# Sorted block attention and a token mixer on one core: first V regrouped, half of a q loaded in fp32, X of two batches turned by transposing transfers, another order

## The chip, the cores and the metric

The kernel runs on one core of one Trainium2 chip. A core has TensorE (PE), VectorE (DVE), ScalarE (ACT), GpSimd (POOL) and SyncE (SP), and 16 DMA engines that all queues share. The metric is device microseconds of one execution. A profiled execution has a span, from its first to its last recorded event, that is a little shorter than its time.

## The reference

```python
P = sort_net                                     # [4, 8, 8, 8]
for _ in range(5):
    P = exp(P - max(P, -1)); P = P / sum(P, -1); P = P / sum(P, -2)
k_sorted = einsum('bhij,bhjcd->bhicd', P, k_b)   # k, v: [4, 8, 768, 64], in 8 blocks of 96 rows
v_sorted = einsum('bhij,bhjcd->bhicd', P, v_b)
attn = softmax(q_block @ k_sorted_block.T / sqrt(64))      # inside each block of 96
x = (attn @ v_sorted_block)                      # to [4, 768, 512]
wq, wk = x @ w_q, x @ w_k                        # [4, 768, 64]
mixed = (wq @ wk.T / sqrt(64)) @ x
out = relu(mixed) @ w_out                        # [4, 768, 512] fp32
```

## The kernel before

Everything is kept on chip between the loads of q, k, v (four batches, 1.5 MB of fp32 each, cast to bf16 by Pool's transfers on the way) and the stores of `out`. Each engine runs its instructions in the order in which they are written, and that order is one hand-held list, the string ORDER. An entry is a letter for the step, a digit for the batch, then the part; after colons the engine (A ACT, D DVE, G Pool, S SyncE) and the PSUM bank. A capital letter is a step on TensorE (except D, R, N), the small letter the step that takes its result out of PSUM. So `Q21:0` turns part 1 of q of batch 2 into bank 0, and `q21:D` copies it to QT on DVE. Waits follow from the data, so an entry that waits holds all later entries of its engine, and of no other.

The steps, with the number of matmuls on TensorE:
- `a`, `c` (L171, L183): five rounds of the sinkhorn on 32x64 values, ACT and DVE in turn; `B` (L234) and `n` (L244) spread the result to the sort matrices M, by DVE for batch 0 and by Pool (1.3 us each) for the others. `Z` (L256): matmuls on zeros, no result.
- `l` (L220): loads, issued by Pool: `lq0` is q of batch 0, and `lq0b` its upper half. Three buffers each for q, k, v. `lp` the two small weights, `lo` w_out (wo).
- `Q` (12 matmuls) turns q; `K` (12) sorts and turns k. `S` (10, the last part 4) scores, `e` their exponentials E on ACT (L350).
- `V` (8, L303) sorts v into Vs; `R` (L313), a transfer by SyncE, regroups Vs from 6 rows per partition to blocks, in VT: six transfers per batch. In the kernel before, batch 0 goes without R: `Y` (12, L288) sorts v as K does, `y` copies it to a spare KT, `F` (8, L294) turns it back and `f` copies it to VT.
- `P` (14, the last part 8): attention times VT; `r` the reciprocals of the row sums, `x` (L378) the multiply that writes X, [96, 4 pairs of heads, 8 blocks, 128].
- `T` (8, L390) turns one quarter of X, `t` copies it to XT. `J` (4, L397) multiplies all four quarters of XT by w_q and w_k together: one J needs all of XT, for half of the columns. `j`, `d` (L405; by SyncE a transfer, by DVE a copy) put the results at qkT and qD.
- `W`, `G`, `H` (4 each for W and H, 8 for G): wk, the product wk.T @ x, then the mixed rows, two of six per H; `h` the relu into mixT.
- `O` (4 matmuls of 128x128x512, L453) one of six output rows; `o` its copy to `ot` (four buffers of two rows); `s` (L466) the store by SyncE, of two rows at once (512 KB) for batches 0 to 2 and of one (256 KB) for batch 3.

The function `u_D` (L386, `D`) writes half of XT by one transposing transfer; no entry of the order before uses it. With SPQ False, lines 128 to 132 and the first branch of `u_z` are not used either. After the last step Pool checks the row sums (L479) and falls back to a general path that does not run here.

Loads in the order before: q0, k0, v0, v1, k1, q1, the weights, q2, k2, v2, q3, k3, v3, w_out. The last batch ends with `O33:4 o33:A:4 s33:S`.

Of the kernel before, what the change touches and what calls it, by code (L numbers as in the profile page):

```python
# [12 lines left out]
ACT = mybir.ActivationFunctionType  # L13

NMIX = 2
SPQ = False
SPLIT = 6

ORDER = """
i02:D lq0 i00:G c00:D a01:A c01:D A00:0 a02:A:0 c02:D a03:A Z09:0 Q00:0 c03:D Q01:1 a04:A c04:D lk0  # L20
a05:A Q03:7 Q02:6 q01:A:1 c05:D Z06:2 B00:1 n00:D:1 n01:D:1 Z02:2 K00:2 K01:4 q00:A:0 k00:A:2
n02:D:1 u00:D:1 i03:G n03:D:1 K03:0 K02:2 k01:A:4 k02:D:2 k03:A:0 S00:4 S02:0 e00:A:4 q02:D:6 lv0
e02:A:0 Y02:2 q03:D:7 Y01:4 lv1 Y00:6 y01:D:4 Y03:0 y02:A:2 S04:2 y00:A:6 lk1 lq1 n10:G n11:G y03:D:0 S03:4
F01:6 F00:7 e04:A:2 S01:0 F03:2 e03:A:4 e01:A:0 f01:D:6 f00:D:7 V11:3 V12:5 f03:D:2 F02:7 P00:0
v11:A:3 v12:D:5 S05:2 f02:A:7 e05:A:2 r00:D:0 V10:4 n21:G P01:6 K13:2 x00:D:0 r01:D:6 P02:0
x01:D:6 v10:A:4 r02:D:0 K10:4 K12:6 k13:A:2 P03:2 x02:D:0 r03:D:2 k10:A:4 K11:4 k12:D:6 T01:0
T00:1 lp Q11:6 k11:A:4 t00:A:1 S06:4 U00:7 R12:S Q12:1 R15:S e06:A:4 R11:S x03:D:2 P04:2 t01:D:0
Q13:0 Q10:4 q11:A:6 r04:D:2 z01:A:7 S12:5 q12:D:1 x04:D:2 q13:A:0 U01:7 q10:D:4 z02:D:7 T02:1 T03:0
e12:A:5 t02:D:1 t03:D:0 lq2 S11:2 S10:4 S13:6 Q22:1 Q21:0 e11:A:2 q21:D:0 Q23:2 e10:A:4 q22:D:1
J00:3 e13:A:6 R10:S R14:S n20:G R13:S S16:4 e16:A:4 S15:0 j00:D:3 P11:6 S14:3 J01:5 e15:A:0 q23:D:2  # L30
e14:A:3 P12:0 r11:D:6 lk2 K23:2 j01:A:5 x11:D:6 K21:6 r12:D:0 P13:4 k23:A:2 K20:2 x12:D:0 k21:A:6
r13:D:4 n30:G K22:0 Q20:6 x13:D:4 W00:7 k20:A:2 lv2 k22:A:0 P14:2 lq3 V20:4 V22:0 d00:S q20:D:6
r14:D:2 W01:7 x14:D:2 V21:2 T12:6 v22:D:0 t12:D:6 v20:A:4 P10:4 S25:0 v21:A:2 S26:2 T13:6 r10:D:4
w00:A:7 T11:7 x10:D:4 d01:S e26:A:2 S23:2 n31:G e25:A:0 Q30:4 G00:5 S21:0 t13:D:6 e23:A:2 t11:D:7
S24:6 lk3 e21:A:0 G01:5 Q31:3 lv3 e24:A:6 g00:D:5 Q33:2 q31:D:3 S22:0 T10:5 e22:A:0 S20:6 q33:D:2
t10:D:5 K32:2 R21:S K31:0 J11:5 k32:A:2 R20:S q30:D:4 R22:S H00:2 Q32:4 e20:A:6 k31:D:0 lo j11:D:5
h00:A:2 R23:S K30:0 R24:S H01:6 q32:D:4 K33:4 h01:A:6 R25:S k30:D:0 P21:2 J10:0 V31:6 k33:A:4 P23:4
j10:A:0 v31:A:6 r21:D:2 P22:0 d10:S x21:D:2 r23:D:4 V32:2 W10:6 v32:A:2 W11:6 O01:7 x23:D:4 w10:A:6
V30:4 r22:D:0 v30:A:4 x22:D:0 o01:D:7 O02:2 S34:0 o02:D:2 H02:6 e34:A:0 h02:D:6 S32:3 O03:5 e32:A:3
o03:A:5 P20:0 T21:7 P24:2 r20:D:0 T22:4 t21:A:7 G10:5 G11:5 x20:D:0 r24:D:2 d11:S g10:D:5 S36:6  # L40
R32:S t22:A:4 S30:0 e36:A:6 R35:S O00:4 x24:D:2 S31:5 e30:A:0 R30:S H11:2 H10:0 O05:7 o00:D:4 T20:4
h11:D:2 o05:D:7 e31:A:5 R34:S T23:5 h10:A:0 t20:A:4 t23:A:5 S35:2 e35:A:2 R31:S S33:0 H12:6 e33:A:0
s01:S O04:4 J20:5 O10:3 s00:S j20:A:5 R33:S P31:0 J21:5 o10:A:3 P32:2 h12:D:6 O15:6 r31:D:0 o04:D:4
j21:A:5 r32:D:2 o15:A:6 x31:D:0 P33:4 r33:D:4 O12:7 o12:A:7 P30:0 x33:D:4 s02:S O13:6 d20:S P34:4
W20:7 x32:D:2 W21:7 r34:D:4 d21:S o13:A:6 T31:2 w20:D:7 O14:3 t31:D:2 r30:D:0 O11:7 G20:2 x30:D:0
G21:2 o11:A:7 s10:S x34:D:4 T30:7 o14:A:3 g20:A:2 t30:A:7 T32:0 T33:1 t32:D:0 t33:D:1 H21:4 H20:2
H22:6 h20:D:2 s11:S J30:0 J31:1 h22:D:6 O20:2 j30:D:0 O21:3 h21:A:4 W30:0 O22:7 j31:A:1 d31:D
w30:A:0 W31:0 o22:D:7 w31:D:0 O24:1 o20:A:2 o21:A:3 o24:A:1 G30:7 G31:7 g30:D:7 O23:0 d30:D H30:4
h30:A:4 o23:D:0 H31:2 s12:S h31:D:2 O25:7 s20:S H32:0 s21:S O31:4 o25:A:7 h32:D:0 O30:7 o31:D:4
s22:S s31:S O34:1 o34:A:1 o30:D:7 O32:4 O35:0 o32:A:4 s30:S o35:A:0 s34:S s32:S s35:S O33:4 o33:A:4  # L50
s33:S
"""


# [1 line left out]
def kernel(  # L56
# [12 lines left out]
    B, H, S, D = q.shape  # L69
    NB = sort_net.shape[-1]  # L70
    BLK = S // NB
# [7 lines left out]
    DM = moe_w_out.shape[0]  # L79
# [21 lines left out]
    def tiles(name, n, shape, dtype=BF16):  # L101
        return [sb.tile(shape, dtype, name=f"{name}{i}") for i in range(n)]

    PS = psp.tile([P, 8, 512], FP32, name="ps")
    ENG = {"A": nc.scalar, "D": nc.vector, "G": nc.gpsimd, "S": nc.sync}
# [13 lines left out]
    X = tiles("X", 2, [BLK, NP, NB, P])  # L119
    XT = tiles("XT", 2, [P, PT, S])  # L120
# [6 lines left out]
    ot = tiles("ot", NOT, [P, 2, DM], FP32)  # L127
    if SPQ:

        q32 = XT[0].rearrange("p t s -> p (t s)").bitcast(FP32).rearrange("p (h r d) -> p h r d", r=R6, d=D)  # L130
        nc.sync.dma_start(out=q32.rearrange("p h r d -> p h (r d)"),
                          in_=q[0, 0:H // 2].rearrange("h (p r) d -> p h (r d)", p=P))
# [251 lines left out]


    def u_D(b, n, e, bank):  # L386
        ENG[e].dma_start(out=XT[b % 2][:, 2 * n:2 * n + 2, :].rearrange("p k (i c) -> p (k i) c", c=BLK),
                         in_=X[b % 2][:, 2 * n:2 * n + 2].rearrange("c k i m -> c (k i m)"), transpose=True)

    def u_T(b, n, bank):  # L390
        for i in range(NB):
# [56 lines left out]
    def osplit(b, n):  # L448

        r, m = n % 10, n // 10  # L450
        return (r, slice(m * DM // 2, (m + 1) * DM // 2)) if b == B - 1 and r >= SPLIT else (r, slice(0, DM))

    def u_O(b, n, bank):  # L453
        r, c = osplit(b, n)
        for t in range(PT):
            mm(PS[:, bank, c], mixT[b % NMIX][:, t // 2, t % 2, r, :], wo[:, t, c],
               start=(t == 0), stop=(t == PT - 1))

    def oslot(b, n):
        return ot[(b * 3 + n // 2) % NOT]  # L460

    def u_o(b, n, e, bank):
        r, c = osplit(b, n)
        copy(e, oslot(b, r)[:, r % 2, c], PS[:, bank, c])

    def u_s(b, n, e, bank):  # L466
        od = out[b].rearrange("(p r) e -> p r e", r=R6)
        if b < B - 1:
            ENG[e].dma_start(out=od[:, 2 * n:2 * n + 2, :], in_=oslot(b, 2 * n))
        else:  # L470
            r, c = osplit(b, n)
            ENG[e].dma_start(out=od[:, r, c], in_=oslot(b, r)[:, r % 2, c])
# [172 lines left out]
    for item in ORDER.split():  # L645
# [5 lines left out]
        b, n = int(name[1]), int(name[2:])  # L651
# [41 lines left out]
```

## Time and profile before

| | us |
|---|---|
| median of 3 runs | 105.38 (105.36 to 105.59) |
| the profiled execution | 105.29 |
| its span | 103.5 |
| busy: PE, weight load, DVE, ACT, POOL | 86.7, 60.3, 71.8, 69.2, 25.4 |
| matmuls of O, 89 recorded | 22.8 busy, 380 ns each |
| copies to XT: ACT (6), DVE (10) | 808 and 544 ns each |
| regrouping transfers R, 18: issue on SP, to landing | 0.59 median; 2.3 to 7.5, median 6.2 |
| span over time in 40 slices, DMA busy | near full from 5 to 58 us, then 2 to 7 tenths |

PE's busy time counts each matmul with its pipeline, so a merged row of 16 matmuls is not twice as long as one of 8. The time to landing of a transfer runs from its issue to its last byte, and includes what stands ahead of it in its queue: the Pool's loads are issued some 10 to 25 us before they land, in one queue. A name such as VT stands for all buffers of that name.

### The profile page before, as it was taken

What the parts mean: (1) busy time and instruction counts of PE and PEld (TensorE: products, weight loads), DVE (VectorE), ACT (ScalarE), POOL (GpSimd) and SP (SyncE); (2) the same over time, 40 slices, a digit from 0 to 9 for tenths busy, and PEclk for the clock granted to TensorE, in tenths of its full rate; (3) what the DMA queues carried; (4) which work ended last, traced back from release to release, by engine and by line L of the source; (5) the groups of instructions that cost most, each with busy time, mean ns of one, the idle gap of its engine ahead of it and who ended that gap; (6) DMA issues with size and microseconds to landing.
All of it is one profiled execution on the core that took longest, in us unless ns stands there. A gap on an engine that the chain in (4) does not pass through costs nothing.

```text
span 103.5 us, 3508 instructions
## 1 busy us (share of the span) xinstructions
PE 86.7 (84%) x1485; PEld 60.3 (58%) x1493; DVE 71.8 (69%) x142; ACT 69.2 (67%) x98; POOL 25.4 (25%) x42
## 2 busy tenths in 40 slices
PE   0297977996959699999969899999999999999930
PEld 0135366895838577898745675856667575543410
DVE  2676667889956578989559498777389979368400
ACT  4222479998668868979849688989944282633440
POOL 5992054991199500000000000000000272000000
PEclk9999999999999999999999999999999999999999
DMA  0899999999999999999999933737042077047782
GB/s 3 88 199 204 204 204 205 203 206 203 237 232 244 206 202 204 209 210 206 241 247 228 208 77 100 224 142 255 6 176 65 6 301 307 24 185 301 299 321 99
DMA packets 18593, 19.35 MB, mean 187 GB/s; under 512 B 912, under 2 KB 16656, under 8 KB 18576
## 3 DMA queue, kind: packets, MB, share of 16 engines
q0 software_dynamic: 13296, 10.09, 63.6%
q1 hardware_dynamic: 5280, 9.03, 25.2%
q8 instruction: 11, 0.18, 0.7%
q14 instruction: 6, 0.05, 0.1%
HBM read 20.19 MB, written 6.29 MB: 256 GB/s over the span
## 4 chain that ended last, share of the span: by engine, by line
PE 44%; DMA 39%; POOL 6%; ACT 3%; SPq 2%; issue 2%; POOLq 0%; ACTq 0%
PE ps L156 44%; DMA Kn<-in_k_dram 18%; DMA Vn<-in_v_dram 14%; DMA VT<-Vs 7%; SPq L314 2%; POOL Vn L231 2%; POOL M L252 1%; POOL Qn L231 1%; ACT Vs L160 1%; POOL Kn L231 1%; ACT KT L160 1%; ACT ot L160 1%; POOL E L211 1%; ACT wk L160 0%; POOL VT L217 0%
## 5 line engine op out<-in xcount | busy, mean ns | idle before, releaser
L352 ACT ACTIVATE E<-ps 96x960 bf16<-96x960 f32 (+1 forms) x28 | 23.9, 905 | 2.9 <-PE ps L156 2.9
L156 PE MATMUL ps<-wo,mixT 128*128 128x512 bf16 x89 | 22.8, 380 | 0.5 <-issue 0.2
L381 DVE TENSOR_TENSOR X<-ps,Rall 96x896 bf16<-96x896 f32 (+1 forms) x20 | 19.9, 1001 | 0.5
L160 ACT COPY ot<-ps 128x512 f32<-128x512 f32 (+1 forms) x16 | 9.2, 587 | 8.6 <-PE ps L156 8.0
L160 ACT CAST KT<-ps 128x768 bf16<-128x768 f32 x14 | 10.6, 806 | 4.9 <-PE ps L156 4.9
L156 PEld LDWEIGHTS <-mixT 128*128 128x128 bf16 x96 | 8.3, 98 | 9.1 <-issue 1.0
L484 POOL CROSS_LANE_REDUCE s<-Rall 96x1 f32<-96x280 f32 x1 | 0.8, 756 | 46.5 <-DVE Rall L376 46.5
L156 PE MATMUL ps<-VT,E 96*128 96x65 bf16 x256 | 11.4, 193 | 0.8 <-DMA VT<-Vs 0.7
L156 PEld LDWEIGHTS <-E 96*128 96x128 bf16 x256 | 9.9, 97 | 3.1 <-issue 0.8
L252 POOL TENSOR_TENSOR M<-PTR,m_p 128x512 bf16<-128x512 bf16 x6 | 7.8, 1314 | 11.6 <-PE ps L156 6.0
L156 PEld LDWEIGHTS <-KT 64*128 64x128 bf16 (+1 forms) x288 | 8.3, 97 | 3.5 <-issue 2.2
L156 PE MATMUL ps<-QT,KT 64*128 64x96 bf16 x256 | 9.2, 204 | 0.4 <-ACT KT L160 0.3
L156 PE MATMUL ps<-idb,Qn 128*64 128x128 bf16 x192 | 7.1, 221 | 2.6 <-DMA Qn<-in_q_dram 2.6
L446 DVE TENSOR_SCALAR mixT<-ps 128x1024 bf16<-128x1024 f32 x7 | 8.5, 1220 | 1.2 <-PE ps L156 0.7
L156 PE MATMUL ps<-M,Kn 128*64 128x128 bf16 x192 | 7.2, 221 | 2.4 <-DMA Kn<-in_k_dram 1.8
L376 DVE RECIPROCAL Rall<-ps 96x14 f32<-96x14 f32 (+1 forms) x20 | 4.6, 231 | 6.7 <-PE ps L156 5.5
L156 PEld LDWEIGHTS <-Qn 128*64 128x64 bf16 x192 | 5.9, 110 | 4.0 <-DMA Qn<-in_q_dram 3.3
L156 PEld LDWEIGHTS <-Kn 128*64 128x64 bf16 x192 | 6.0, 109 | 3.7 <-DMA Kn<-in_k_dram 2.6
L160 ACT CAST Vs<-ps 128x1024 bf16<-128x1024 f32 x7 | 7.1, 1014 | 1.4 <-PE ps L156 1.2
L162 DVE COPY QT<-ps 128x768 bf16<-128x768 bf16 x12 | 6.3, 545 | 2.0 <-PE ps L156 2.0
L162 DVE CAST KT<-ps 128x768 bf16<-128x768 f32 x6 | 5.6, 942 | 2.8 <-PE ps L156 2.8
L162 DVE COPY ot<-ps 128x512 f32<-128x512 f32 x9 | 6.0, 678 | 2.1 <-PE ps L156 2.1
(81 smaller groups left out, 132.1 us busy)
## 6 DMA issues: line engine op xcount, KB each, us to landing
out_dram<-ot SPq DMA_DIRECT2D x9, 512.0 KB, 2.9
Qn<-in_q_dram POOLq DMA_DIRECT2D x4, 768.0 KB, 16.3
Kn<-in_k_dram POOLq DMA_DIRECT2D x4, 768.0 KB, 17.6
Vn<-in_v_dram POOLq DMA_DIRECT2D x4, 768.0 KB, 14.8
VT<-Vs SPq DMA_DIRECT2D x18, 132.0 KB, 6.2
out_dram<-ot SPq DMA_DIRECT2D x6, 256.0 KB, 2.0
wo<-in_moe_w_out_dram POOLq DMA_DIRECT2D x1, 512.0 KB, 26.7
qD<-qkT SPq DMA_DIRECT2D x6, 48.0 KB, 2.3
```

The source lines that it names most:

```text
L156: nc.tensor.matmul(o, w, x, is_transpose=t, start=start, stop=stop, skip_group_check=True)
L160: nc.scalar.copy(o, i)
L162: nc.vector.tensor_copy(o, i)
L211: nc.gpsimd.memset(t[:, :, 2 * TH * BLK:EW], 0.0)
L231: nc.gpsimd.dma_start(out=t[b % NIN][:, h0:h1].rearrange("p h r d -> p h (r d)"), in_=src[b, h0:h1].rearrange("h (p r) d -> p h (r d)", p=P))
L252: ENG[e].tensor_tensor(out=M[b % 2][:, h0:h0 + hn], in0=src.unsqueeze(2).to_broadcast([P, hn, SP, NB]), in1=m_p.unsqueeze(1).unsqueeze(3). ...
L314: ENG[e].dma_start(out=VT[b % 2].rearrange("(s r) i h x -> r s i (h x)", r=R6)[n], in_=Vs[0][:, n].rearrange("p h e -> p (h e)"))
L352: nc.scalar.activation(E[b % 2][:, n, 0:2 * w * BLK].rearrange("p (t a c) -> p a t c", a=2, c=BLK), PS[0:BLK, bank:bank + 2, 0:w * BLK].re ...
L376: nc.vector.reciprocal(Rall[:, b, n, :, 0:w], avps(bank, w)[:, :, :, D])
L381: nc.vector.tensor_mul(xo.rearrange("p (a t d) -> p a t d", a=2, d=D), avps(bank, w)[:, :, :, 0:D], Rall[:, b, n, :, 0:w].unsqueeze(3).to_ ...
L446: nc.vector.tensor_relu(o, i)
L484: g.tensor_reduce(s1[:, 1:2], rv, axis=AX.XYZWC, op=ALU.max)
```

## The change

`SPQ` is set: SyncE loads the first four heads of q of batch 0 in fp32, into the space of XT of batches 0 and 2, before anything else but `sort_net`; `z11` and `z10` cast it on ACT to Qn, and Pool loads the other half (`lq0b`). Batch 0's v goes through `V` and `R` like the others, so `Y`, `F` and their copies are gone. `T` and `t` of batches 2 and 3 (eight of each) are gone; `D20`, `D21`, `D30`, `D31` on SyncE turn two quarters of X each. Stores of batches 0 and 1 go out by single rows (`ROWS`), and rows 0 and 1 of batch 3 by one store at the very end (`s320`). `SPLIT` splits nothing before or after. The whole order is another one.

```diff
-SPQ = False
-SPLIT = 6
+SPQ = True
+SPLIT = ()
+XK = 2
+ROWS = ((0, 0), (0, 1), (0, 2), (1, 0), (1, 1), (1, 2))
...
-i02:D lq0 i00:G c00:D a01:A c01:D A00:0 a02:A:0 c02:D a03:A Z09:0 Q00:0 c03:D Q01:1 a04:A c04:D lk0
...
+i02:D c00:D lk0 a01:A c01:D i00:G A00:2 a02:A:2 z11:A c02:D Z08:2 Q01:2 a03:A z10:A c03:D a04:A
+c04:D a05:A c05:D Q00:1 i03:G lq0b Z09:0 B00:5 n03:D:5 n00:D:5 lv0 n01:D:5 Z03:0 K00:3 k00:D:3 lq1
...
+n30:G V22:2 r12:D:0 v22:A:2 P10:4 S25:6 x12:D:0 J00:0 r10:D:4 x10:D:4 V21:2 e25:A:6 V20:4 j00:A:0
+v21:D:2 P13:0 K30:6 v20:A:4 k30:A:6 K31:2 r13:D:0 d00:S K33:4 x13:D:0 k31:A:2 K32:6 T12:0 P11:1
+k33:D:4 R20:S t12:D:0 P14:3 k32:A:6 S23:5 R25:S r14:D:3 x14:D:3 r11:D:1 J01:7 R22:S e23:A:5 j01:A:7
+W00:0 R21:S R23:S S24:3 Q30:5 x11:D:1 Q31:6 e24:A:3 W01:0 q30:D:5 T11:1 Q32:2 lv3 q31:A:6 T10:4
+w00:D:0 t11:A:1 T13:7 q32:D:2 S30:5 S21:2 S31:0 t13:D:7 R24:S G00:7 G01:7 t10:A:4 J10:4 e30:A:5
+g00:D:7 lo e21:A:2 e31:A:0 j10:D:4 J11:5 V30:2 j11:D:5 v30:A:2 V31:0 v31:D:0 d01:S V32:4 P24:2
+r24:D:2 H00:6 H01:0 R32:S v32:A:4 P20:4 x24:D:2 W10:2 h00:A:6 Q33:3 r20:D:4 h01:A:0 W11:2 P21:6
...
+G11:3 S35:1 R33:S g10:A:3 R35:S S34:6 R31:S P22:4 O00:3 d11:S r22:D:4 e34:A:6 e35:A:1 P23:6 O04:0
+x22:D:4 o00:A:3 R34:S r23:D:6 o04:A:0 x23:D:6 O05:3 H11:6 H10:0 o05:D:3 D20:S S33:4 h11:A:6 O01:2
+e33:A:4 P30:6 o01:A:2 h10:D:0 P31:0 D21:S r31:D:0 s00:S P32:4 O03:2 J20:3 o03:A:2 r30:D:6 s01:S
+x30:D:6 j20:A:3 O11:6 s02:S o11:A:6 r32:D:4 x31:D:0 W20:3 x32:D:4 J21:0 d20:S P33:1 j21:A:0 d21:S
+S36:6 H12:4 W21:3 e36:A:6 w20:A:3 r33:D:1 x33:D:1 O12:0 P34:6 h12:A:4 G20:3 G21:3 O13:4 o13:A:4
+o12:D:0 r34:D:6 O14:5 D30:S g20:A:3 x34:D:6 D31:S O10:6 o14:A:5 H20:0 H21:2 h20:A:0 o10:D:6 s11:S
+H22:4 O15:7 h21:A:2 J31:6 j31:D:6 d31:D h22:A:4 s10:S o15:D:7 J30:1 O22:3 j30:D:1 W31:6 O23:2 W30:1
...
+O35:7 o33:A:0 o32:A:1 s33:S s32:S o35:A:7 O31:1 s35:S o31:A:1 o34:D:6 O30:7 s34:S o30:A:7 s320:S
...
-        ENG[e].dma_start(out=XT[b % 2][:, 2 * n:2 * n + 2, :].rearrange("p k (i c) -> p (k i) c", c=BLK),
-                         in_=X[b % 2][:, 2 * n:2 * n + 2].rearrange("c k i m -> c (k i m)"), transpose=True)
+        t = slice(XK * n, XK * n + XK)
+        ENG[e].dma_start(out=XT[b % 2][:, t, :].rearrange("p k (i c) -> p (k i) c", c=BLK),
+                         in_=X[b % 2][:, t].rearrange("c k i m -> c (k i m)"), transpose=True)
...
-        if b < B - 1:
-            ENG[e].dma_start(out=od[:, 2 * n:2 * n + 2, :], in_=oslot(b, 2 * n))
+        if b < B - 1 or n >= 20:
+            m = 2 * (n % 20)
+            w = 1 if (b, n) in ROWS else 2
+            for r in range(0, 2, w):
+                ENG[e].dma_start(out=od[:, m + r:m + r + w, :], in_=oslot(b, m)[:, r:r + w, :])
```

The loads come in the order k0, upper half of q0, v0, q1, k1, v1, q2, k2, the weights, v2, k3, q3, v3, w_out.

## The prediction

> **What bounds the kernel now.** I read the chain of waits first, in order of time.
>
> ```profile
> 6.63 18.26 DMA Kn<-in_k_dram
> ...
> 29.34 14.51 DMA Vn<-in_v_dram
> ...
> 49.73 7.52 DMA VT<-Vs
> ...
> 86.39 6.24 PE ps L156 x51
> 92.62 0.16 issue
> 92.78 6.56 PE ps L156 x31
> ```
>
> Start, length, what. Until 57.26 the chain goes from landing to landing; from there it is TensorE in pieces without a gap worth naming. Busy time by engine in three windows cut at that place says the same.
>
> ```profile
> 0.00:57.30 57.30, 45.22 (x984) 34.92 (x985) 41.88 (x96) 41.80 (x58) 22.22 (x35) 1.00 1.21 199
> 57.30:99.40 42.10, 41.43 (x501) 25.34 (x508) 29.90 (x46) 26.78 (x40) 3.22 (x7) 1.00 0.51 172
> 99.40:103.50 4.10, 0.00 (x0) 0.00 (x0) 0.00 (x0) 0.59 (x1) 0.00 (x0) 0.95 0.44 168
> ```
>
> Columns: window and length, busy PE, weight load, DVE, ACT, POOL, granted clock, DMA share, GB/s. In the first window TensorE is idle for 12.1 us and the transfers run at 199 GB/s (bytes as written; the casting loads read twice that). In the second it is idle for 0.7 us of 42.1 at clock 1.00. The third is the last copy and store. So three terms set the end: when the last operand lands, TensorE's work after that, and the tail.
>
> The waits of TensorE and the sizes and landing times of the transfers:
>
> ```profile
> PE ps L156 <- DMA Qn<-in_q_dram: 2.6, 3, 1.0
> PE ps L156 <- DMA Kn<-in_k_dram: 1.8, 2, 1.0
> PE ps L156 <- DMA VT<-Vs: 0.7, 1, 0.7
> ```
> ```profile
> out_dram<-ot SPq DMA_DIRECT2D x9, 512.0 KB, 2.9
> Qn<-in_q_dram POOLq DMA_DIRECT2D x4, 768.0 KB, 16.3
> VT<-Vs SPq DMA_DIRECT2D x18, 132.0 KB, 6.2
> out_dram<-ot SPq DMA_DIRECT2D x6, 256.0 KB, 2.0
> ```
>
> **The stream of loads, priced.** Issue plus time to landing of each load gives: Q0 9.0, K0 12.85, V0 16.6, V1 20.8, K1 24.9, Q1 29.5, the two small weights 30.9, Q2 35.8, K2 39.6, V2 43.9, Q3 47.8, K3 53.1, V3 58.35, wo 60.9. Undisturbed neighbours are 3.75 to 3.9 us apart (Q0 to K0, K0 to V0, Q2 to K2). From Q0 to V3 lie 11.17 loads in 49.4 us; 11.17 x 3.8 is 42.4, so 6.9 us went to the 12 regroupings (R) and two qD transfers among them, and to irregular steps (V0 to V1 took 4.2 with no R). I take 0.49 us for an R, 2.9 for six.
>
> **TensorE's items, priced** by how much longer a merged row is with one more of them (X turned: 8 matmuls 0.51, 16 0.85, 24 1.19, so 0.34 for a T): Q and K 0.33, V 0.46, S 0.21 (S.6 0.08), P 0.43 (P.4 0.25), T 0.34, J 0.65, W 0.17, G 0.43, H 0.23, O 0.865. From P21, which starts on the last landing at 57.39, the order before holds 10 P, 5 J, 3 V, 6 W, 24 O, 7 S, 10 H, 8 T, 6 G: 39.3 us. The trace took 41.95 (to 99.34). The factor is 1.067.
>
> **The change part by part.**
>
> *First V regrouped.* Four Y and four F (3.2 us of TensorE) and their eight copies (0.7 to 1.0 us each) become three V (1.4 us), three copies (1.0 to 1.2) and six R. The engine time saved lies in the first window, where TensorE has 12 us to spare: worth nothing now, and should the loads cease to bind, at most the 1.8 us of TensorE. The six R join the stream ahead of V3: +2.9 us. If the VT transfers filled only holes it would be 0, but the DMA share of 1.2 to 1.33 from 5 to 58 us shows none.
>
> *Half of the first q in fp32.* SP issues it second (about 1.15 us; the sort_net transfer issued at 0.75 landed at 2.3). The Pool stream moves its first bytes at 3.0 and full rate only at 5.0; until then it moved 0.19 MB, as if it had begun at 4.0. Half a load is 1.9 us of stream. Nearly all of it now runs in idle time: -1.5 us, bounds 0 (it merely shares) and -1.9. On ACT two casts to Qn (0.8 each, as the 128x768 copies) stand between the exponentials of the sinkhorn, where ACT idles 1.46 to 1.52 us per round. The first waits for the transfer, and the next exponential stands behind it; I expect landing near 5.9, so the matrix is some 0.4 us late. Its readers (M, then K00) then come at 13 instead of 12.5, against loads that are ahead of TensorE: hidden. Uncovered it would be 0.4. Pool issues K0 first and half of Q0 after the memsets: the same bytes.
>
> *Order.* V1 moves behind Q1 and K1, Q3 behind K3; V3 stays last but wo. TensorE now meets V30 where it met P21: VT of batch 2 is issued by 52.5 and lands, as before after about 7 us, near 59.5, when three V are still to run. V3 lands at 58.35 - 1.5 + 2.9 = 59.75. The work ahead of V30 is no later: from V22 (V2 lands near 45.0) to Q30 are 6.7 us of items, Q3 lands near 54.2, from Q30 to V30 are 5.0 x 1.067 = 5.3, which gives 59.5. Pool's four M products still stand ahead of loads; the last of them queue behind V12's reads of M, near 32 us, when 12 us of loads are in flight: hidden.
>
> *X of batches 2 and 3 turned by transposing transfers.* Eight T (2.7 us) and eight copies (0.55 DVE, 0.81 ACT) leave. From V30 the new order holds 3 V, 10 P, 12 H, 6 W, 1 Q, 24 O, 5 S, 6 G, 4 J: 36.3, x 1.067 = 38.7. TensorE would end at 98.5 instead of 99.34: -0.85, if nothing waits. Against it stands J, which needs all of XT. After x23, the multiply that D21 waits for, TensorE has work until J20 worth 4.5 x 1.067 = 4.8 us; after x34, from which D31 starts, 4.0 us (P34 to J31 holds 5.0 of items, x34 ends 1.6 after P34, J31's first two matmuls read the other half).
>
> No row shows a transposing transfer. It moves 384 KB on the chip in 1536 pieces of 256 B. Lower bound: as a store, between 2.0 (256 KB) and 2.6 (the quietest 512 KB), 2.4 us: no wait. Upper bound: every piece a load packet (63.6% of 103.5 us x 16 / 13296 = 79 ns), 96 per engine 7.6 us, and 2.0 to land: 9.6. The nearest row is R, the other on-chip regrouping: three R carry the bytes. Three issues of 0.588 and a landing of 2.35 (R on the quiet queue at 60 to 62 us) are 4.1; with the 4.3 that they took beside stores, 6.1. The queue is quiet here, so 4.6. D20 holds SP for some 1.76 us and starts D21 about 0.35 late: D21 is 4.6 + 0.35 - 4.8 = 0.15 late, D31 0.6: +0.75. The queue behind D20 and D21 holds stores and d20, d21, which wait for J anyway.
>
> The Trainium skill (Advanced Engine Details and Errata, X-Bar Transpose) says that transposing transfers are as fast as ordinary ones. By that rule the sum loses its 0.75. The Trainium skill (DMA: Bandwidth & Descriptors, the table of sequencer costs) counts 32 sequencer cycles per tile on earlier generations; 96 tiles of 16x128 at the 1.2 GHz of the clock table (Advanced Engine Details, Clock Domains) would be an estimate of 2.6 us of issue each, and with a landing of 2.35 the two waits together 2.2 instead of 0.75: 107.5. No run here shows either yet.
>
> *Stores.* Batches 0 and 1 go out by rows: six more issues of 0.33 us, on an SP queue that waits 5 us at a time for copies: hidden. The very last store becomes 512 KB instead of 256: 2.6 to 2.9 against 2.0, +0.7, at the end of everything.
>
> Sum: -0.85 + 0.75 + 0.7 = +0.6. The profiled execution took 105.29, 1.8 more than its span (the median is 105.38). 105.29 + 0.6, and a little for waits behind new neighbours: **106.0**.
>
> **Rivals.**
> - *Faster: transposes within their cover.* At up to 4.0 us neither J waits. With the other terms as above that is 105.14; with the first q fully ahead (-1.9), R at 0.35 (2.1) and the tail at 0.3, V3 lands at 58.55, TensorE ends at 97.3, and the time is 103.5. It decides where x34 to the landing of D31 is under 4.0. For it: the quiet queue after 62 us; against: 1536 small pieces. This is also where the skill's rule leads. 0.37 for a gain, 0.12 for 105.17 to 105.6.
> - *Slow transposes.* At 7 to 9.6 us D21 comes 2.5 to 5.1 late and D31 3.0 to 5.6: 111 to 116. For it: the packet price; against: that price belongs to loads that read 1536 B. 0.10.
> - *The stream is later than I add*, with q shared rather than ahead: V3 at 61.2, +1.5: 107.4, within my case.
> - *The change does nothing it says*: possible for the first two parts, which then cost and gain 0; the transposes still move T off TensorE. Within the range.
>
> **How the numbers follow.** The forecast case, slower by 0.2 to 3.5 us, holds 0.41; with slow transposes slower is 0.51. Measurements of this kernel tell about 0.2% apart, 0.2 us. Same 0.12, faster 0.37. Cases of both signs hold most of the chance: the forecast's own range is 105.6 to 108.9; the whole, leaving out the slow end of the transposes and the best end of the gain, 103.4 to 109.5.
>
> **What would show it.** Landing of V3 (59.75) and the first V30 matmul on it; TensorE busy without gaps from there except ahead of J20 and J31, with "DMA XT<-X" as releaser and 0.15 and 0.6 us; time to landing of XT<-X near 4.6; TensorE's last matmul near 99.3; last store to landing 2.6 to 2.9. Wrong would be: landing of XT far from 4.6, a wait of several us on VT or Qn after 60 us, or V3 before 58.4.

## The result, and the profile after

The changed kernel takes 106.6 us, median of 4 runs (106.43 to 107.49), against 105.37 of the kernel before beside it: ratio 1.0112, interval 1.007 to 1.0153. It is slower by a good 1%. The profiled execution took 106.43 with a span of 104.6; before it was 105.29 and 103.5.

The chain of waits after the change, its last part (start, length, what):

```profile
53.84 8.67 DMA VT<-Vs
62.51 0.24 issue
62.75 10.34 PE ps L156 x177
73.08 3.53 DMA XT<-X
76.61 0.04 issue
76.66 23.81 PE ps L156 x188
```

Before, the last landing on the chain was at 57.26. Now a VT landing at 62.5 and a transposing transfer stand on it, 5 us and 19 us later. The windows, cut where the first V of batch 3 begins on TensorE (60.27) and where TensorE ends (columns as before: window and length, busy PE, weight load, DVE, ACT, POOL, clock, DMA share, GB/s):

```profile
0.00:60.27 60.27, 47.09 (x936) 36.09 (x937) 38.31 (x88) 45.56 (x62) 22.18 (x35) 0.97 1.22 213
60.27:100.50 40.23, 39.03 (x442) 22.88 (x439) 26.73 (x42) 25.36 (x39) 3.22 (x7) 1.00 0.72 207
100.50:104.60 4.10, 0.00 (x0) 0.00 (x0) 0.00 (x0) 0.57 (x1) 0.00 (x0) 1.00 0.58 231
```

The same cut in the kernel before is at 58.67, where its first V of batch 3 begins:

```profile
58.67:99.40 40.73, 40.18 (x485) 24.43 (x489) 29.56 (x45) 26.15 (x39) 3.22 (x7) 1.00 0.48 171
```

So the 1.1 us are made up thus: V of batch 3 begins 1.6 us later; the part from there to TensorE's end is 0.5 shorter (40.2 for 40.7: 1.15 us less of work, 0.65 more of idle time); the tail is the same 4.1. The two stretches do not hold quite the same items: behind V30 there are eight T and two S fewer than behind the first V of batch 3 before, and a P, a Q and two H more. Of the 1.15 us of work saved, more than half came back as idle time. These are the waits of TensorE (us in total, times, longest):

```profile
PE ps L156 <- DMA Kn<-in_k_dram: 2.4, 1, 2.4
PE ps L156 <- ACT E L352: 1.2, 4, 0.4
PE ps L156 <- DMA VT<-Vs: 1.0, 1, 1.0
...
PE ps L156 <- DMA XT<-X: 0.2, 1, 0.2
```

The 1.0 and the 0.2 are the only named waits behind 60 us: P24 on VT of batch 2 (at 62.75) and J20 on the transposes (at 76.66). The 2.4 is K of batch 1, which keeps TensorE from 22.96 to 25.37 (before, it waited 0.84 for that load); its granted clock falls behind it. The time before V of batch 3 shows where the start was lost. From 20 to 50 us and from 50 to 60, before and then after:

```profile
20.00:50.00 30.00, 26.52 (x630) 22.52 (x628) 23.36 (x40) 25.02 (x33) 10.67 (x12) 1.00 1.30 214
50.00:60.00 10.00, 8.22 (x183) 6.14 (x180) 6.81 (x12) 7.53 (x10) 0.00 (x0) 1.00 1.22 227
```
```profile
20.00:50.00 30.00, 23.37 (x540) 19.80 (x542) 18.60 (x29) 24.60 (x32) 12.74 (x14) 0.94 1.28 222
50.00:60.00 10.00, 9.83 (x224) 8.11 (x224) 7.74 (x15) 9.35 (x13) 0.00 (x0) 1.00 1.26 231
```

Before, TensorE got 26.5 us done from 20 to 50 and had room from 50 to 60. After, it got 23.4 done and was full from 50 on: the work was pushed back and met V of batch 3 as a queue. Transfers, from issue to landing:

```profile
VT<-Vs SPq DMA_DIRECT2D x24, 132.0 KB, 6.4
...
XT<-in_q_dram SPq DMA_DIRECT2D x1, 768.0 KB, 4.5
...
XT<-X SPq DMA_TRANSPOSE x4, 3.8
```

Landings, issue plus time to landing: K0 9.6, half of Q0 11.5, V0 15.4, Q1 20.2, K1 25.3, V1 30.6, Q2 34.4, K2 39.0, V2 45.6, K3 49.6, Q3 53.2, V3 59.3, wo 62.7. Before, V2 came at 43.8, V3 at 58.4, wo at 60.9.

### The profile page after: what moved, and what is told of

Read it like the earlier page. It is cut to its first block, busy times and chain, and to the rows that moved or that the text cites. A ratio compares the mean times of both kernels' runs of the same rounds, so it can differ in the third digit from the quotient of the medians.

```text
span 104.6 us, 3280 instructions
## 1 busy us (share of the span) xinstructions
PE 86.1 (82%) x1376; PEld 59.0 (56%) x1376; DVE 65.0 (62%) x129; ACT 71.5 (68%) x100; POOL 25.4 (24%) x42
## 4 chain that ended last, share of the span: by engine, by line
PE 44%; DMA 30%; DVE 8%; POOL 5%; ACT 5%; issue 4%; SPq 1%; DVEq 0%; POOLq 0%; ACTq 0%
PE ps L156 44%; DMA Kn<-in_k_dram 18%; DMA VT<-Vs 8%; DVE X L381 4%; DMA XT<-X 3%; ACT KT L160 2%; DVE KT L162 2%; POOL Qn L231 2%; ACT E L352 1%; SPq L314 1%; POOL Kn L231 1%; ACT Vs L160 1%; DVE Vs L162 1%; POOL Vn L231 1%; DVE Rall L376 1%
## 5 line engine op out<-in xcount | busy, mean ns | idle before, releaser
L160 ACT CAST Vs<-ps 128x1024 bf16<-128x1024 f32 x10 | 10.0, 1018 | 2.4 <-PE ps L156 1.6
L156 PE MATMUL ps<-M,Kn 128*64 128x128 bf16 x192 | 8.0, 226 | 4.1 <-DMA Kn<-in_k_dram 2.4
L445 ACT ACTIVATE mixT<-ps 128x1024 bf16<-128x1024 f32 x8 | 7.9, 1023 | 3.8 <-PE ps L156 3.8
L162 DVE CAST KT<-ps 128x768 bf16<-128x768 f32 x8 | 7.5, 952 | 4.5 <-PE ps L156 4.5
L156 PE MATMUL ps<-idb,Qn 128*64 128x128 bf16 x192 | 8.4, 239 | 0.9 <-DMA Qn<-in_q_dram 0.7
L156 PEld LDWEIGHTS <-KT 64*128 64x128 bf16 x256 | 7.1, 99 | 3.7 <-issue 1.8
L160 ACT CAST KT<-ps 128x768 bf16<-128x768 f32 x8 | 6.1, 801 | 4.2 <-PE ps L156 4.2
L156 PEld LDWEIGHTS <-Qn 128*64 128x64 bf16 x192 | 6.6, 121 | 2.5 <-DMA Qn<-in_q_dram 0.9
L156 PE MATMUL ps<-fil 128*128 128x512 bf16 x20 | 6.5, 480 | 1.6 <-ACT m_p L174 1.6
L156 PE MATMUL ps<-Vn,M 128*128 128x128 bf16 x96 | 7.1, 219 | 0.9 <-ACT E L352 0.5
```

The source lines that it names most:

```text
L156: nc.tensor.matmul(o, w, x, is_transpose=t, start=start, stop=stop, skip_group_check=True)
L160: nc.scalar.copy(o, i)
L162: nc.vector.tensor_copy(o, i)
L445: nc.scalar.activation(o, i, ACT.Relu)
```

## The experiments

Each is timed beside the kernel before on the same chip (medians 105.44 for e1 to e4, 105.54 for e5 to e11, 105.65 for e12).

| run | us, median (range) | ratio to before | interval |
|---|---|---|---|
| the change | 106.6 (106.43 to 107.49) | 1.0112 | 1.007 to 1.0153 |
| e1, filler ahead of K10 | 106.07 (105.86 to 106.14) | 1.0054 | 1.0037 to 1.0071 |
| e2, change without R of batch 0 | 107.99 (107.5 to 108.96) | 1.0226 | 1.0195 to 1.0258 |
| e3, change with T on TensorE | 112.7 (112.64 to 112.84) | 1.0692 | 1.067 to 1.0714 |
| e4, change with q by Pool | 107.62 (107.12 to 108.61) | 1.0226 | 1.016 to 1.0293 |
| e5, e1 with V of batch 2 early | 106.58 (106.37 to 107.85) | 1.0105 | 1.007 to 1.014 |
| e6, e1 with a divided last store | 106.35 (106.03 to 107.42) | 1.0062 | 1.0032 to 1.0093 |
| e7, before with D20, D21 | 105.65 (105.42 to 106.27) | 1.0001 | 0.9973 to 1.0028 |
| e8, e7 with D30 | 105.71 (105.36 to 106.34) | 1.0003 | 0.9976 to 1.0031 |
| e9, before with half of q in fp32 | 105.02 (104.91 to 105.81) | 0.9964 | 0.9944 to 0.9984 |
| e10, before with six R too many | 107.79 (107.58 to 108.09) | 1.0216 | 1.0192 to 1.0241 |
| e11, e9 with D20, D21 | 104.08 (103.9 to 105.14) | 0.9886 | 0.9851 to 0.9921 |
| e12, e11 with D30 | 104.85 (104.58 to 105.7) | 0.9933 | 0.9906 to 0.9961 |

**e1: the clock behind the wait for K of batch 1.** Ten matmuls on zeros fill the wait (in the entry `Z010:5` the 10 is their number and the 5 the bank).

```diff
-K10:6
+Z010:5 K10:6
```

> The changed kernel with ten matmuls on zeros (Z) in the wait for K1, nothing else. Theory clock: in the changed kernel TensorE idles 2.4 us before K10 and its granted clock falls to 0.5 from about 27 to 30.6 us; the late V of batch 2, so its R and VT (landing 62.5), follow from that. Then the clock stays at 1.00, the items from K10 to P00 run some 1.8 us sooner, V1 (30.6) binds instead, and the time falls by 0.5 to 1.0 us, to 105.6 to 106.1, with less spread between runs. Theory stream: the six added R make the stream longer and that alone sets VT's landing. Then the clock is mended and the time stays within 0.2 us of 106.5.

The windows of the changed kernel around the wait; the number behind POOL is the granted clock:

```profile
23.00:24.00 1.00, 0.00 (x0) 0.00 (x0) 0.49 (x2) 1.00 (x3) 1.00 (x3) 1.00 1.23 241
24.00:25.00 1.00, 0.00 (x0) 0.00 (x0) 0.00 (x0) 0.88 (x2) 1.00 (x2) 1.00 1.21 248
...
27.00:28.00 1.00, 0.88 (x18) 0.83 (x20) 0.83 (x1) 0.33 (x2) 0.00 (x0) 0.56 1.21 245
28.00:29.00 1.00, 1.00 (x26) 0.83 (x24) 0.47 (x1) 0.91 (x2) 0.00 (x0) 0.50 1.33 215
29.00:30.00 1.00, 1.00 (x25) 0.86 (x22) 0.09 (x1) 0.69 (x2) 0.00 (x0) 0.50 1.29 199
30.00:31.00 1.00, 0.72 (x21) 0.58 (x16) 0.55 (x1) 1.00 (x2) 0.00 (x0) 0.73 1.34 207
```

and of e1:

```profile
24.00:25.00 1.00, 1.00 (x6) 0.47 (x5) 0.00 (x0) 1.00 (x2) 1.00 (x3) 1.00 1.23 250
...
28.00:29.00 1.00, 0.81 (x32) 0.60 (x28) 0.67 (x2) 1.00 (x2) 0.00 (x0) 1.00 1.32 215
```

With the gap filled the clock stays at 1.00, and the median is 0.5 us lower (the intervals of the two just meet, at 1.007). The five runs lie within 0.3 us, where the changed kernel's four spread over 1.1. But VT of batch 2 still lands at 62.4, so that landing does not hang on the clock. And in the profiled executions the mended clock is not seen behind the loads: V30 begins at 60.27 in the change and at 60.47 with the filler, and P24 at 62.75 in both. The two lines of e1:

```profile
60.47 1.50 PE L156 MATMUL ps<-Vn,M 128*128 128x128 bf16 x24
62.75 0.41 PE L156 MATMUL ps<-VT,E 96*128 96x65 bf16 x8 [0.77 <-DMA VT<-Vs]
```

TensorE ends 0.34 us earlier with the filler. All of that comes at J20, which waits for D21 in the change and not with the filler, where D20 held SyncE for 1.66 us instead of 2.28. The changed kernel's other three executions had mean clocks of 0.942 to 0.961 (the profiled one 0.984) and took 106.43 to 107.49 us. These three have no profile, so how much of the 0.5 us is the clock's stays open.

**e2: R of batch 0 taken out of the change** (Y, y, F, f of batch 0 in place of V, v, R).

```diff
-V02:0 v02:A:0 V01:2 v01:A:2
+Y02:0 y02:A:0 Y01:2 y01:D:2
...
-R03:S R05:S lv1
+lv1
...
-S03:0 R02:S R04:S e04:A:2 K10:6 q11:D:4
+S03:0 Y03:6 y03:D:6 e04:A:2 F02:5 f02:D:5 q11:D:4 F01:4 f01:D:4 F00:5 f00:A:5 F03:4 f03:D:4 K10:6
```

> The changed kernel with the first V regrouped on TensorE again (Y, y, F, f in place of V, v and six R of batch 0; the four F lie in the wait for K1). Theory stream: six R cost 2.9 us of stream, so Q1 to V3 land 2 to 3 us sooner, V3 near 56.5, VT of batch 2 near 59.5, and the time falls by 1.5 to 2.5 us, to 104 to 105, under the kernel before. Rival: the chain after K1 is bound by engines, not by the stream; then V3 lands sooner but the time falls by less than 0.8 us.

V3 landed at 56.9, 2.4 earlier, and V2 at 43.7, 1.9 earlier. Yet the time rose by 1.4: the eight steps were put by hand into an order searched without them, and TensorE waits 1.6 us for the copy to QT that now stands among theirs on DVE; its clock falls behind that wait too, from 25.9 to 29.3. The landing answers the price of the six R (2.4); the time does not answer what the part is worth.

**e3: transposes back on TensorE**, in the places of the transfers.

```diff
-D20:S
+T20:2 t20:D:2 T21:3 t21:A:3
...
-D31:S O10:6 o14:A:5
+O10:6 o14:A:5 T32:7 t32:A:7 T33:3 t33:D:3
```

> The changed kernel with the four transposing transfers undone: eight T on TensorE and eight copies. Theory: the transfers land 3.5 to 4.8 us after issue, inside their cover, and take 2.7 us off a TensorE that is busy throughout; undone, the time rises by 2.0 to 2.8 us, to 108.5 to 109.2. Rival, as forecast: waits at J eat part of that, then it rises by 1 to 1.9 us.

+6.1 us, more than either bound. From V30 to its last product TensorE takes 46.1 us instead of 40.2: 3.2 more of work, which is the eight T, and 2.7 more of idle time. The longest new wait is not that of a T:

```profile
88.16 1.02 PE L157 MATMUL ps<-wo,mixT 128*128 128x512 bf16 x4 [1.24 <-DVE X L382]
```

It is O10, which takes the bank that x34 has to read first, and x34 now stands on DVE behind the copy of a T. The run shows that the order of the change is laid out for transfers, and not what a T costs in an order made for it.

**e4: all of the first q by Pool.** `SPQ = False`, `lq0` in the place of `lk0` and `lk0` in that of `lq0b`, no `z10`, `z11`.

> The changed kernel with the whole first q loaded by Pool (cast on the way), ahead of k0, and no casts on ACT. Theory: the fp32 half is worth 1.5 us of stream; all landings come 1.5 us later (V1 32.1, V3 60.8), and the time rises by 0.7 to 1.5 us, to 107.2 to 108. Rival: the chain behind K1 is bound by engines; then the time rises by less than 0.4 us.

The loads from Q1 on land 0.5 to 1.0 us later (V2 46.3, V3 60.0, wo 63.7), and the time rises by 1.0. The fp32 half is worth 0.8 us of stream at V3, half of what the forecast gave it.

**e5: V of batch 2 early**, so that VT lands before P24 wants it.

```diff
-V22:2 r12:D:0 v22:A:2 P10:4 S25:6 x12:D:0 J00:0 r10:D:4 x10:D:4 V21:2 e25:A:6 V20:4 j00:A:0
-v21:D:2 P13:0 K30:6 v20:A:4 k30:A:6 K31:2 r13:D:0 d00:S
+V22:2 r12:D:0 v22:A:2 P10:4 V20:6 v20:A:6 x12:D:0 V21:2 v21:D:2 J00:0 R20:S R25:S R22:S R21:S
+R23:S R24:S r10:D:4 x10:D:4 j00:A:0 S25:6 e25:A:6 P13:0 K31:2 K30:6 k31:A:2 k30:A:6 r13:D:0 d00:S
```

> The changed kernel with the filler of e1, and with V20 and V21, their copies and all six regrouping transfers of batch 2 put forward, ahead of S25, P13 and the K3 items. My theory: what the changed kernel loses after 52 us starts from VT of batch 2, which lands at 62.4 because V20's copy ends at 50.6 and the six R's are issued from 50.6 to 54.9; put forward, the last R is issued about 1.5 us earlier, VT lands near 61 and the wait of P24 (1.0 us) goes: 0.5 to 1.0 us below e1, near 105.3, with the changed kernel at 106.6 and e1 at 106.1. Rival (the end is set by the sum of TensorE's items behind the last load V3, the wait being only moved): V3 still lands at 59.3, TensorE is busy at the same places, and the time stays within 0.2 us of e1.

The change and e5 at this place on TensorE (start, length, items, and in brackets the idle time before and what ended it). The change:

```profile
60.27 1.50 PE L156 MATMUL ps<-Vn,M 128*128 128x128 bf16 x24
...
62.75 0.41 PE L156 MATMUL ps<-VT,E 96*128 96x65 bf16 x8 [0.98 <-DMA VT<-Vs]
```

e5:

```profile
52.27 0.53 PE L156 MATMUL ps<-M,Kn 128*64 128x128 bf16 x12 [0.69 <-ACT KT L160]
...
61.18 1.50 PE L156 MATMUL ps<-Vn,M 128*128 128x128 bf16 x24
...
62.93 0.41 PE L156 MATMUL ps<-VT,E 96*128 96x65 bf16 x8 [0.25 <-ACT Vs L160]
```

The wait for VT is gone, and P24 starts 0.2 us later than with it. The copies of V put forward on ACT hold up the copies of K3, TensorE waits 0.69 for one of them, and V of batch 3 begins at 61.18 instead of 60.27 (e1: 60.47). The time is 106.58, 0.5 above e1 and 0.2 above e6, which has the same filler and was timed beside it. My theory falls: taking the wait away gained nothing, because P24 then met the queue in which TensorE stands from 50 us on (busy 9.83 of 10 us in the change, with ACT at 9.35). The edit also lengthened that queue; VT earlier with the copies left in place was not tried, so what the wait costs by itself is not shown.

**e6: the last store divided**, in e1.

```diff
-O31:1 s35:S o31:A:1 o34:D:6 O30:7 s34:S o30:A:7 s320:S
+O31:1 s35:S o31:A:1 s31:S o34:D:6 O30:7 s34:S o30:A:7 s30:S
```

> The changed kernel with the filler of e1, rows 0 and 1 of the last batch stored in two transfers of 256 KB instead of one of 512 KB. By the forecast's term (the joint last store adds 0.7 us behind the last copy) this is 0.7 us below e1, 105.4. By the traces of before and after, in which 3.5 us lie behind the last product in both, it is within 0.2 us of e1.

106.35 against 106.07 of e1, with overlapping intervals: nothing gained. The joint 512 KB at the end cost nothing measurable. The profiled execution of e6 (107.42, the longest of twelve) shows the clock fall once more, at another place (from 41.1 to 47.9), though no wait there was longer than 0.63 us:

```profile
39.00:40.00 1.00, 0.54 (x17) 0.39 (x14) 0.00 (x0) 0.90 (x1) 1.00 (x2) 1.00 1.30 244
...
41.00:42.00 1.00, 1.00 (x21) 0.78 (x18) 0.95 (x2) 0.59 (x1) 0.14 (x1) 0.56 1.23 249
42.00:43.00 1.00, 1.00 (x18) 0.86 (x20) 0.14 (x1) 0.00 (x0) 0.00 (x0) 0.50 1.22 249
...
47.00:48.00 1.00, 1.00 (x20) 1.00 (x18) 0.08 (x1) 1.00 (x2) 0.00 (x0) 0.53 1.31 209
```

**The parts one by one in the order of before.** e2 and e3 show that undoing a part in a searched order mixes its price with that of a misfit. So the other way round: one part at a time into the kernel before.

e7, X of batch 2 by transfers: `T20` to `T23` and their copies out, and

```diff
-h10:A:0 t20:A:4 t23:A:5 S35:2 e35:A:2 R31:S S33:0
+h10:A:0 S35:2 e35:A:2 R31:S R33:S D20:S D21:S S33:0
...
-J20:5 O10:3
+O10:3 J20:5
```

> The kernel before with one part of the change alone: X of batch 2 turned by two transposing transfers, not by its four T's on TensorE and their copies; R33 stands ahead of them on SyncE, and O10 ahead of J20. If the transposing transfers cost only what J20 waits for them, as the trace of the changed kernel suggests (issue 1.4 to 2.3 us, landing within 4.8 us, a wait of 0.2 us), four T's of 0.34 us leave TensorE behind V3: -1.3 us, near 104.1. By the forecast's own terms for this part, +0.1 to +0.6 of wait in place of it: 104.2 to 104.7. Rival, the transfers are what makes the changed kernel slow (J20 waits 2 us and more, or the R's of batch 3 queue behind them on SyncE): 105.4 or above.

(R33 moves ahead of them on SyncE.) No gain, 105.65. J20 did not wait for the transfers, which landed within 3.9 us. TensorE's busy time from 60 to 80 us before, and in e7:

```profile
60.00:80.00 20.00, 19.78 (x301) 13.30 (x301) 15.42 (x24) 16.06 (x23) 0.00 (x0) 1.00 0.40 132
```
```profile
60.00:80.00 20.00, 18.78 (x270) 12.19 (x271) 15.33 (x23) 13.38 (x19) 0.00 (x0) 1.00 0.58 173
```

TensorE is idle there for 1.2 us instead of 0.2. So of the 1.4 us that left it, 1.0 came back as idle time, in pieces of 0.2 and 0.3 us (some of the waits from 55 us on):

```profile
PE ps L155 <- issue: 0.5, 3, 0.2
PE ps L155 <- DMA wo<-in_moe_w_out_dram: 0.3, 1, 0.3
PE ps L155 <- ACT ot L159: 0.2, 1, 0.2
PE ps L155 <- DVE mixT L445: 0.2, 1, 0.2
```

The 0.3 is O02's, ahead of the part in question: wo came late in this execution. The two waits for a copy are products that take a bank which the copy has still to read (G10 that of o03, S35 that of h11); before, T's stood between. The pieces called issue have no releaser in the profile, so for them this is not shown.

e8, e7 with `D30` in place of `T30`, `T31` and their copies, behind `x30`:

> e7 with half of X of batch 3 turned by a transposing transfer as well, in place of T30 and T31 and their copies. If the transfer lands before J30 and J31 want it, a further 0.34 to 0.68 us below e7 (near 103.6); if it lands late behind the stores on SyncE's queue, J31's wait takes the gain back: within 0.3 us of e7, or above it.

105.71, no further gain; J30 waited 1.24 us for the transfer (TensorE's waits, the line on XT):

```profile
PE ps L155 <- DMA XT<-X: 1.2, 1, 1.2
```

e9, half of the first q in fp32 (`SPQ = True`), with what goes with it: K of batch 0 is first in Pool's queue, and Q02 and Q03 stand behind the fillers.

```diff
-i02:D lq0 i00:G c00:D a01:A c01:D A00:0 a02:A:0 c02:D a03:A Z09:0 Q00:0 c03:D Q01:1 a04:A c04:D lk0
-a05:A Q03:7 Q02:6 q01:A:1 c05:D Z06:2 B00:1
+i02:D lk0 i00:G lq0b c00:D a01:A c01:D A00:0 a02:A:0 z11:A c02:D a03:A z10:A Z09:0 Q01:0 c03:D Q00:1
+a04:A c04:D a05:A q01:A:0 c05:D Z06:2 Q03:7 Q02:6 B00:1
```

> The kernel before with one part of the change alone: the first half of q of batch 0 in fp32 by SyncE with two casts on ScalarE, K of batch 0 first on GpSimd's queue, Q02 and Q03 behind the fillers. In e4 taking this part out put V3 0.7 and wo 1.1 later. Theory (the kernel before is bound by the landing of V3 and wo): V3 near 57.6 instead of 58.4, wo near 60.0 instead of 60.9, and 0.7 to 0.9 us off the time, near 104.7. Rival (TensorE's own queue or the late transposed Pb decides): within 0.3 us of before.

V3 landed at 57.6, wo at 60.1, each 0.8 earlier, and the median fell by 0.5 us.

e10, six R too many, on an order otherwise untouched:

```diff
+        if b == 0:
+            ENG[e].dma_start(out=VT[1].rearrange("(s r) i h x -> r s i (h x)", r=R6)[n],
+                             in_=Vn[0].rearrange("p h r d -> p (h r d)")[:, 0:H * DV])
+            return
...
-F01:6
+R03:S R05:S R02:S R04:S R00:S R01:S F01:6
```

> The kernel before with six regrouping transfers too many: like the change's R of batch 0 in size, shape and queue (SyncE), but from columns of V of batch 0 as it lands, into VT of batch 1, which the true R of batch 1 write later; nothing else is moved. It prices the stream's share of the first part alone. By the forecast, 0.49 each: V3 lands 2.9 us later (61.3) and the time is 2.5 to 2.9 us longer, near 108. By e2, where their removal put V3 2.4 us earlier: V3 near 60.8, time near 107.8. Rival (regrouping transfers fill gaps of the stream and cost it little): V3 within 1 us of 58.4, time below 106.5.

V3 landed at 61.4 and wo at 64.0, 3.0 and 3.1 later; the time rose by 2.3 us. The six transfers as the profile lists them (issue on SyncE, in ns, least, median, most; first and last start):

```profile
L315 SPq DMA_DIRECT2D VT<-Vn x6: 598/600/694, 16.7 to 20.0; - x6
```

The stream pays 0.5 us for each of these 132 KB. Here too TensorE ran at clock 0.50, from 25.9 to 32.7, in and behind the longer wait for K1 (24.2 to 27.4). It leaves no trace at the end: O02 still starts as wo lands, and the part behind it is as long as before (the table after e12).

e11, e9 and e7 together:

> e9 with X of batch 2 turned by transposing transfers as in e7. If what held e7 back was the landing of V3 and wo in front (wo at 61.6 there, O02 waits for it), earlier loads let it gain: 0.3 to 0.7 us below e9. If it is the engines' copies between the products (ACT's, DVE's and TensorE's own queue waits, 1 us of new waits in e7 from 62 to 80), e11 is within 0.2 us of e9.

104.08: 0.9 below e9 and 1.5 below before, the fastest of all. By my expectation that would make the landings in front the cause of e7's nothing; the trace says less (below, after e12).

e12, e11 with e8's part and O11 put behind H22:

```diff
-O14:3 t31:D:2 r30:D:0 O11:7 G20:2 x30:D:0 G21:2 o11:A:7
+O14:3 r30:D:0 G20:2 x30:D:0 D30:S G21:2
...
-H22:6 h20:D:2 s11:S J30:0 J31:1
+H22:6 O11:7 h20:D:2 o11:A:7 s10:S s11:S J30:0 J31:1
```

> e11 with half of X of batch 3 turned by a transposing transfer as in e8, in place of T30 and T31, and O11 put behind H22, so that J30 has a product of 0.86 us ahead of it that does not need the transfer. In e8 J30 waited 1.24 us for XT and the part gained nothing. Theory (the transfer is worth its two T's, 0.7 us, less what J30 waits): the wait falls to 0.4 us or less, and the time is 0.3 to 0.7 us below e11, near 103.6. Rival (J30's wait stays, or the copies of the G and H products now stand in the way): within 0.2 us of e11, or above it.

In this order O11 writes its product to bank 7, the second of the two banks that H22 has just filled, before h22 has read them; half of rows 4 and 5 of batch 2 is thus not the reference's. The amount of work is not changed by it, but h22 now waits 0.50 us on DVE for ACT's o11. 104.85, 0.8 above e11 (the two intervals overlap a little). J30 still waited:

```profile
85.01 1.47 PE L155 MATMUL ps<-XT,wqk 128*128 128x384 bf16 x8 [0.81 <-DMA XT<-X]
```

The product put in front could not help: D30 is issued at 81.50, as x30 ends, and lands 3.47 us later, at 84.97. In e11, whose O02 starts 0.53 earlier, J30 starts at 83.76. So J30 starts 0.7 later, counted from O02, whatever TensorE does meanwhile.

These six kernels keep the order of before behind 60 us but for what they change, and can be laid side by side. In all of them O02 starts as wo lands (within 0.1 us, in e8 and e12 0.4); three lines on O02 show it, of before, e9 and e10:

```profile
60.95 1.02 PE L156 MATMUL ps<-wo,mixT 128*128 128x512 bf16 x3
```
```profile
60.19 1.03 PE L156 MATMUL ps<-wo,mixT 128*128 128x512 bf16 x3
```
```profile
64.03 1.02 PE L156 MATMUL ps<-wo,mixT 128*128 128x512 bf16 x3 [0.32 <-DMA wo<-in_moe_w_out_dram]
```

| profiled execution | before | e9 | e10 | e7 | e11 | e8 | e12 |
|---|---|---|---|---|---|---|---|
| O02 starts | 60.95 | 60.19 | 64.03 | 61.63 | 60.06 | 61.73 | 60.59 |
| TensorE's last product ends | 99.34 | 98.59 | 102.43 | 99.70 | 98.13 | 100.56 | 99.38 |
| between | 38.39 | 38.40 | 38.40 | 38.07 | 38.07 | 38.83 | 38.79 |
| from there to the end of the span | 4.2 | 4.5 | 3.7 | 4.5 | 4.0 | 3.9 | 3.8 |

The middle row takes the landings out. The loads change nothing behind O02 (38.4 three times). X of batch 2 by transfers saves 0.3 us, with and without the fp32 half; half of X of batch 3 loses 0.7 or 0.8, in both. That loss is the landing of D30: counted from O02, J30 starts 0.7 us later in e12 than in e11 and 0.8 later in e8 than in e7. What is left between e7 and e11 is the start and the tail, which differ from execution to execution: e7's wo came 0.7 later than before's, though nothing ahead of it had changed. The profiled execution of e7 (106.07) is also 0.4 above its median, and that of e11 (103.90) the shortest of six. One profile of each can't say how much of e11's 0.9 is steady. Its median of 104.08 was measured; that the transfers earn more than 0.3 of it was not shown.

## Why the prediction was right, and where it was not

The time forecast was 106.0, the side was right, and 106.6 lies in the forecast's own range. Point by point:

- *The bound* (last landing, then TensorE's work, then the tail) holds in the order of before: e9 and e10 move the landings alone by -0.8 and +3.1, TensorE's end follows by -0.75 and +3.1, and the time, with tails of 3.7 to 4.5 us, by -0.5 and +2.3. In the changed kernel it does not hold: V3 lands at 59.25, and V30 begins 1.0 us later.
- *Six R, +2.9 of stream.* e10 measured 3.0. Right.
- *Half of the first q in fp32, -1.5.* Its landing (5.7, forecast 5.9) and the late sinkhorn (hidden) were right. The size was not: e4 and e9 give 0.8 at V3, a little under midway between the bounds of 0 and 1.9. At V0 the gain is still 1.2 in both, and 0.4 of it is gone by V3; where, no run separates.
- *V3 lands at 59.75.* 59.3. Right in the sum, with the smaller q made up by something that no run separates: the parts' own sizes, 58.4 + 3.0 - 0.8, would give 60.6. The other sequence of loads may do it; it was not tried.
- *"VT of batch 2 is issued by 52.5 and lands ... near 59.5"* failed by 3.0 us: issued from 50.6 to 54.9, landed at 62.5, the last R in 8.7 us where I took 7. P24 waits 1.0 us for it. e5 takes that wait away and gains nothing, but with V30 0.9 later.
- *"The work ahead of V30 is no later"* failed by 0.5 (60.27 for 59.75), though V3 had landed at 59.25. This step lies under the other too, for V21 and V20, whose copies the R's wait for, stand in the same queue. The forecast put 6.7 us of items between V22 and Q30 and 5.0 between Q30 and V30, with 2.5 us to spare until Q3 lands. These two stretches in the changed kernel:

```profile
46.39:54.51 8.12, 7.94 (x173) 6.66 (x172) 7.61 (x13) 7.14 (x10) 0.00 (x0) 1.00 1.31 206
54.51:60.27 5.76, 5.76 (x122) 4.63 (x119) 3.79 (x7) 5.76 (x8) 0.00 (x0) 1.00 1.22 249
```

  V22 begins 0.8 us after V2 has landed, because TensorE is still at earlier items and then waits 0.27 for an exponential on ACT. Then 11.7 us of items take 13.7 of busy time, a factor of 1.17 where the forecast had at most 1.067. The prices came from merged rows, and here items of different kinds follow one another. Q30 begins at 54.51, though Q3 has landed at 53.2: nothing was left to spare, and V30 began by TensorE's own queue and not by a load. From V22 to V30 TensorE's only named wait for a copy is 0.17 us.
- *TensorE's work from V30, 38.7.* 39.0 busy. Right.
- *Transposes, +0.75.* 0.2 was measured: J20 waited 0.18 (beside e1, where it did not wait, 0.34 was lost), J31 nothing. From the end of x34 to the landing of D31 were 3.9 us; the forecast gave the case to the rival *transposes within their cover* under 4.0. So in this term the rival was right. Time to landing was 3.5 to 4.8, median 3.8, where I took 4.6; issue 1.4 to 2.3 (1.76 forecast). The rule of the Trainium skill (Advanced Engine Details and Errata, X-Bar Transpose), by which this term is nothing, came nearer to what J waited. The transfers themselves took longer than the stores at the end, to land 3.8 us in the median and these 2.7. The estimate of 2.6 us of issue from the Trainium skill (DMA: Bandwidth & Descriptors, the table of sequencer costs) lies above all four.
- *Last store, +0.7.* Nothing: 4.1 us lie behind TensorE's last product before and after, and e6 gains nothing by dividing the store. The store's own time to landing is not all of the tail.
- *Not foreseen: the clock.* K of batch 1 keeps TensorE 2.4 us, and 3.4 us at half clock follow. The filler lowers the median by 0.5 of the 1.2 us, but in the profiled executions neither V30 nor P24 comes earlier with it.

So -0.85 for the end of TensorE became +1.1 (V30 0.5 later, 0.3 more work, 1.2 of waits), +0.75 is within that, and +0.7 for the tail became 0: a sum of nearly the right size in which terms of 0.5 to 1 us cancelled. The side was luck. The two terms that made the forecast slower (+0.75 and +0.7) came to 0.2 and 0; without them the forecast would have been faster, by 0.85. What made the kernel slower is what the forecast had at nothing: 0.5 from TensorE's own queue ahead of V30, the 1.0 that P24 waited, and 0.3 of work.

In the order of before, the parts measured +2.3 (six R, without what Y and F spare), -0.5 (half of q), 0 alone and -0.9 on top of q (X of batch 2, 0.3 of it behind O02), and 0 and +0.8 (half of X of batch 3, 0.7 of it behind O02). The first V regrouped is the one part with a large price, and it is paid in the load stream. The two parts worth having, without it and without the new order, make e11, 104.08, 1.1% faster than before. What the change's own order would give without R of batch 0 stays open: e2 broke the order as it took them out.

## What to carry to other kernels

Work that moves from an engine with spare time into the load stream is paid in full if the stream sets the start of the last stage: six transfers of 132 KB put the last landing 3 us later, and the time 2.3. Work taken off the bound engine is not worth its own length: of 1.4 us of transposes 0.3 were gained, and the rest came back as idle time. Where a load has landed and its reader has not begun, the engine's own queue sets the start, and prices taken from merged rows are too low for it (11.7 us by price took 13.7). And a wait that stands in the chain may only show where a queue stands anyway; take it away before you call it the cause.

## What was not expected of the hardware

TensorE's granted clock fell to 0.50 from 27.1 to 30.5 us, after one idle stretch of 2.4 us. In e10 it fell from 25.9 to 32.7, only 1.7 us into an idle stretch that began at 24.2. And in one execution of e6 it fell from 41.1 to 47.9, after five us in which TensorE was busy 3.7 and never idle for more than 0.63 at once. The Trainium skill (TensorE: Matmul & The Clock Gate, What's actually happening) puts half clock after at least one idle window of about 3.4 us and full clock after at least one busy window as long. The time at half clock agrees: 3.4 us, and in e10 and e6 6.8, twice that. The idle stretches do not: 2.4 us and less were enough here. Ten matmuls on zeros in the wait for K1 kept the clock up in all five runs of e1 (mean 0.995 or more). With the same filler e5 and e6 had executions down to 0.966 and 0.968.

A transposing transfer of 384 KB from [96, 2048] to 16 blocks of [128, 96] held SyncE's queue for 1.4 to 2.3 us and landed 3.5 to 4.8 us after its issue, beside 2.2 to 3.6 for the stores of 256 and 512 KB from 95 us on.
